# Attention, spectral mixing and feed-forward on one core: one written list from the last attention units to the first up-projection

## The chip, the cores and the metric

The kernel runs on one core of a Trainium2 chip, in one launch. The metric is the device time of that launch in microseconds (us). Five engines work side by side: TensorE (PE: matmuls and transposes; PEld: its weight loads), VectorE (DVE), ScalarE (ACT), GpSimd (POOL) and SyncE (SP, which here issues nearly all DMAs). Each has its own stream of instructions and waits for the others by semaphores.

## The reference, cut to what matters

```python
# attention: B=4, H=8, S=576, D=64
scores = q @ k^T / 8 ;  rel = |i - j|
x = log1p(rel) / log1p(max(i, 1))
bias = relu(x*w1 + b1) @ w2                  # hidden 32, one plane per head
attn = softmax(scores + bias) ; a = attn @ v
# mixing and feed-forward: x = a as (4, 576, 512)
u  = x + real(fft(fft(x, axis=seq), axis=feature))
un = (u - mean(u)) / sqrt(var(u) + 1e-6)
out = u + relu(un @ w_ch1) @ w_ch2           # 512 -> 2048 -> 512
```

## The kernel before, in words

**Bias and attention.** A first phase computes the position bias (up to about 65 us). Then come 16 attention units: a unit is a pair of heads of one batch. A unit has nine blocks of 128 score rows. The work of a unit is cut into lettered tokens: `S` scores on PE; `D` adds the bias and takes the row extreme (a custom DVE instruction, line 290); `X` is the exponential on ACT (298); `T`/`R` are PE transposes of the probabilities, `V` their copies out of PSUM; `A` is the product with v (462), `O` copies its result out; `E` transposes that, `Y` scales it by the inverse sums into `x`; `Q` makes those inverse sums (`Q1`, line 486 and 487, also sends a column to other partitions by a DMA, which in the last two units is issued by ACT); `W`/`U` turn a slice of the feed-forward weights into fp32 and store it in device memory. The lists `ORDER` and `SECOND` fix the order on PE, DVE and ACT; a prime means the unit before.

**The passage.** The last unit, the rests of the units before it, and the mixing of batch 0 follow the list `TAIL`, in which PE, DVE, ACT and POOL all stand in written order. Further tokens there: `p`, `g`, `h` fold the sequence (`pq`, `ge`) and split it into a high and a low part (`gh`, `gl`); `z` is the sequence transform (line 674, `zp`, 8 matmuls), `a`/`b` copy its parts out (`z00h`, `z00l`); `f` is the feature transform (693, `abp`, two times 6 matmuls), `i`, `j`, `k`, `l` join it with `x`; `c` is one column (feature 0) for all batches, made by 18 narrow matmuls (827, `cp`) of which the result `dc` enters `j`; `m`, `n`, `r` are the statistics of the norm and its root; `q` calls the square root once so that ACT's table is loaded there (838). The list ends in `E1' O E1`. After it, code that is not in the list scales batch 0 (`un`, lines 778 on ACT and 781 on DVE), transposes it (`ut`, 795), splits it (`uh` on ACT 797, `ul` on DVE 798), and scales the last attention results.

**The feed-forward.** Then no order is written: a scheduler with its own estimates orders the rest. `dense` runs 16 slices f per batch: split `w1` (high part on ACT 886, low part on POOL 887), load and split `w2`, the up-projection (line 909: 4 blocks of 3 matmuls of 512 columns, for f=0 sorted so that the four with `ul` come last), relu split into `hh`/`hl` (914, 915), and one slice later the down-projection (923: 12 matmuls). The mixing and the norm of the next batch run beside it. Batch b+1's folds (654 to 667) run on DVE. Last comes a half batch of the 64 rest rows of all four batches, whose `w2` low parts are made on DVE. `w2` slices are loaded into three buffers in turn.

Of the kernel before, what the change touches and what calls it, by code (L numbers as in the profile page):

```python
# [20 lines left out]
P = 128  # L21
# [4 lines left out]
ND = 258  # L26
# [9 lines left out]
ON_ACT = set("R0 T00 T01 T03 T04 T10 T11 T12 T13".split())  # L36
# [13 lines left out]
A3'' X8' A4'' S1 X2' X4' E1''' R1' D1 S0 Y1''' R0' Q0' VR1' D0 T10' O'' S2 S4 Q1' D2 VR0' T00' VT10'  # L50
T01' VT00' D4 VT01' S3 T11' S6 T02' D3 D6 VT11' E2'' X3 S7 VT02' Y2'' S8 U0 T13' T12' W0 A0' D7 X6 W1 VT13'
W2 W3 S5 T04' VT12' T03' D8 U1 A1' X7 X0 VT03' VT04' X1 D5 U2 U3 X5 A2'
# [5 lines left out]
S1 D1 S2 T10' D2 S4 T00' VT10' T01' D4 VT00' VT01' S8' S3 T11' VT11' D8' X8' T02' D3 S6 Q0' VT02' D6 S0 R1'  # L58
R0' VR1' X3 VR0' D0 S7 S8 U0 T13' T12' W0 A0' D7 X6 W1 VT13' W2 W3 S5 T04' VT12' T03' D8 U1 Q1' A1' X7 X0
VT03' VT04' X1 D5 U2 U3 X5 A2'  # L60
# [5 lines left out]
E1''' c0 X2' A3'' Y1''' X8' p0 X4' A4'' T11' O'' T10' VT11' S2 p1 VT10' W0 T02' D2 U0 S4 Q0' VT02' R0'  # L66
p2 S7 D4 VR0' p3 T03' D7 S8 VT03' T00' D8 S1 VT00' T12' g0 D1 p5 S5 VT12' E1'' X1 p4 S6 Y1'' X7 T04' Q1'
T01' X8 A0' VT01' X2 h0 A1' VT04' g1 D5 T13' D6 X5 S3 R1' X6 S0 VR1' VT13' A2' X4 D0 D3 X0 T11 h1 z00 X3
q W1 z11 W2 U1 c1 T01 a00 A3' a11 Q0 b11 b00 A4' U2 U3 z10 VT11 Q1 VT01 O' W3 T00 a10 R0 b10 z01 VR0
VT00 R1 a01 c2 b01 VR1 f1 c3 T10 i1 T12 VT10 j1 VT12 E2' f0 k1 l1 Y2' T04 m1 i0 T02 VT04 A0 j0 VT02 n1  # L70
T03 l0 E2'' k0 VT03 A1 T13 Y2'' n0 A2 VT13 m0 A3 r A4 E1' O E1
""".split()
TAIL_ACT = set("""
VR0 VR0' VT00' VT01 VT02 VT03 VT03' VT04 VT04' VT10 VT11 VT11' VT12 VT13 VT13'
""".split())
# [14 lines left out]
def shape_tables():  # L90
# [23 lines left out]
    fd[..., 257:] = 0.0  # L114
    return {
# [17 lines left out]
def body(ctx, tc, a, out):  # L133
# [39 lines left out]
    biasp = pool("biasp", 1, stack=early_)  # L173
    smp = pool("smp", 3, stack=late, side="right")
# [3 lines left out]
    pp = pool("pp", 1, stack=late, side="right")  # L178
# [73 lines left out]
    nms, bank = {}, {}  # L252
# [28 lines left out]
    def largest(n, i):  # L281
        hp, b = units[n]
        blk = (BLK if n else BLK0)[i]
        t = blk % 4 if blk < 8 else 4
        if t not in pt_[n]:
            pt_[n][t] = (pp.tile([P, 2, S], F32, tag="p", name="p", bufs=8) if t < 4
                         else pp.tile([P, S], F32, tag="pr", name="pr", bufs=2))
        bias = bt[hp, t][:, blk // 4] if blk < 8 else bt[hp, 4]
        p, bias = (w.rearrange("p (c s) -> p c s", c=2) for w in (prob(n, blk), bias))
        nc.vector.tensor_tensor_reduce(  # L290
            p, bank.pop((n, i))[:, :, :CH], bias, -0.125, 3.0e38, ALU.add, ALU.min, nms[n][:, blk:blk + 1])
        if b == B - 1 and hp + 1 < HP and blk >= 4:
            load_bias(hp + 1, blk - 4)
# [111 lines left out]
    with ExitStack() as st:  # L405
        ptp = pool("ptp", 1, stack=late, side="right")
        otp = pool("otp", 2, stack=late, side="right")
        rawu = pool("rawu", 1, stack=late, side="right")
# [91 lines left out]
        def scaled(u, w):  # L500
# [14 lines left out]
            "T": turn, "R": turn, "V": lambda u, w: turned(u, w[1:], w[1:] in ON_ACT),  # L515
# [87 lines left out]
        def mix_buffers():  # L603
# [7 lines left out]
            fd = fwp.tile([P, 2, 2, 2, ND], F32R, name="fd")  # L611
# [6 lines left out]
        class Mix:  # L618
# [29 lines left out]
            def fold(self, eng, c, i):  # L648

                if i == 0:  # L650
                    self.buffers(c)
# [17 lines left out]
            def seq(self, c, d):  # L669
                gh, gl = self.g[c]  # L670
                ps = self.ps[c, d] = fps.tile([P, 512], F32, tag="f", name="zp")
# [16 lines left out]
            def feat(self, t):  # L688
                ab = self.ab[t] = [fps.tile([P, 512], F32, tag="f", name="abp") for _ in range(2)]
                for c in range(2):  # L690
                    mm = [(z[c, kb][i][:, 128 * t:128 * t + 128], fd[:, kb, c, j]) for kb in range(2) for i, j in PROD]
# [29 lines left out]
            def pieces(self):  # L721
                eng = nc.vector

                def fold(c):
                    for i in range(3):
                        self.fold(eng, c, i)
                    self.fold_hi(c)
                    self.fold_lo(c)

                def seq(c, d):  # L730
                    self.seq(c, d)
                    self.seq_out(c, d, False)
# [12 lines left out]
                return res + [lambda t=t: feat(t) for t in range(2 + self.b % 2)]

        def norm(tiles, act=False):
# [22 lines left out]
            def scale(i):  # L770
                if not un:
                    un.append(unp.tile([P, n, DM], F32, tag="un", name="un"))
                if act and i < 3:
                    if not i:
# [9 lines left out]
            return un, [lambda i=i: stats(i) for i in range(n)], [root] + [lambda i=i: scale(i) for i in range(n)]  # L784

        def flip(un, n):
            ut = []

            def one_tile(t):
                if not ut:  # L790
                    ut.extend(unp.tile([P, 4, 512], F32R, tag=nm, name=nm) for nm in ("uh", "ul"))
                uh, ul = ut
                ps = (fps if t < 2 else hps).tile([P, 4, P], F32, tag="f" if t < 2 else "h", name="ut")
                for kb in range(4):
                    nc.tensor.transpose(ps[:, kb], un[0][:, t, P * kb:P * kb + P], ident)  # L795
                c = slice(P * t, P * t + P)
                nc.scalar.activation(uh[:, :, c], ps, AF.Copy)
                nc.vector.tensor_tensor(ul[:, :, c], ps, uh[:, :, c].bitcast(F32), ALU.subtract)  # L798

            return ut, [lambda t=t: one_tile(t) for t in range(n)]  # L800

# [5 lines left out]
        un, stats, scales = norm(tl, True)  # L807
        root = scales.pop(0)
        col = {}

        def column(i):
# [6 lines left out]
            elif i == 1:  # L818
                cos = col["cos"] = rawp.tile([P, 3, 384], F32, tag="raw", name="cos")
                hi, lo = (fs[:, :, 0, j].bitcast(F32) for j in range(2))  # L820
                nc.gpsimd.tensor_tensor(cos[:, :, 0:320], hi, lo, ALU.add)
                nc.gpsimd.tensor_tensor(cos[:, :, 320:384], hi[:, :, 256:320], lo[:, :, 256:320], ALU.add)
            elif i == 2:
                ps = col["ps"] = tps.tile([P, 3, B], F32, tag="t", name="cp")
                for t in range(3):
                    for kb, p in enumerate((128, 128, 64)):
                        nc.tensor.matmul(
                            ps[:, t], col["cos"][:p, kb, 128 * t:128 * t + 128], col["x"][:p, kb],
                            start=kb == 0, stop=kb == 2)
            else:  # L830
                ps = col["ps"]
                nc.scalar.activation(dc[:, 0:2], ps[:, 0:2], AF.Copy)
# [199 lines left out]
```

## Time and profile before

| | us |
|---|---|
| median of three runs | 786.39 (784.91 to 787.5) |
| the profiled execution, whole | 785.68 |
| its span (first to last instruction) | 783.8 |
| PE busy in the span | 758.9 (97%) |
| ACT / DVE / POOL busy | 436.6 / 433.3 / 345.8 |

The page's rows give for each line an engine's busy time, the mean of one instruction, and the idle time just before it with what ended that. The rows read from it stand below the change.

### The profile page before, as it was taken

Reading aid. Unit: us, or ns where it says so; the run is one execution under the profiler, and the core shown is the slowest. Engines: PE = TensorE matmul, PEld = TensorE weight load, DVE = VectorE, ACT = ScalarE, POOL = GpSimd, SP = SyncE. Lnnn points to the kernel's source line nnn. Section 1 sums busy time; section 2 is a strip of 40 time slices with the busy share of each in tenths; the row PEclk is TensorE's granted clock in tenths of the full one; section 3 lists DMA queues with packets and bytes.
Section 4 is the critical chain, followed back from the end, with each engine's and each line's share of the span. In section 5 each row is a group of like instructions: output and inputs, shape, how many; then the busy total and the mean of one; then the engine's idle time right before and its main releaser. Section 6 shows DMA issues by size and latency. Waiting matters only on the chain.

```text
span 783.8 us, 13206 instructions
## 1 busy us (share of the span) xinstructions
PE 758.9 (97%) x4786; PEld 618.3 (79%) x4786; DVE 433.3 (55%) x962; ACT 436.6 (56%) x901; POOL 345.8 (44%) x293
## 2 busy tenths in 40 slices
PE   6999899999999999979999999999999999999997
PEld 4567677888778887748888888888888888888896
DVE  7997687887887887579471241712228122111433
ACT  7995888877988888554333333333333333333453
POOL 0003554664465644135554434644345444445342
PEclk9999999999999999989999999999999999999999
DMA  8988989989879842541111131111211113111331
GB/s 217 239 221 231 255 218 275 310 233 281 231 208 295 220 123 82 173 163 41 44 38 54 41 95 45 43 48 45 90 55 30 52 43 105 42 53 55 110 98 62
DMA packets 59488, 103.16 MB, mean 132 GB/s; under 512 B 8768, under 2 KB 28864, under 8 KB 58304
## 3 DMA queue, kind: packets, MB, share of 16 engines
q1 hardware_dynamic: 58672, 98.99, 44.7%
q0 software_dynamic: 288, 3.02, 1.1%
q8 instruction: 37, 0.61, 0.3%
q10 hardware_dynamic: 464, 0.33, 0.1%
q14 instruction: 27, 0.22, 0.1%
HBM read 78.58 MB, written 21.07 MB: 127 GB/s over the span
## 4 chain that ended last, share of the span: by engine, by line
PE 84%; DMA 4%; ACT 3%; DVE 3%; issue 2%; SPq 2%; POOL 1%; ACTq 0%; DVEq 0%
PE hp L909 25%; PE acc L923 25%; PE o L462 9%; PE s L272 9%; PE t L441 6%; PE bps L391 2%; PE abp L693 2%; PE zp L674 2%; DMA bias<-ring 1%; DVE hd L371 1%; SPq L330 1%; ACT p L298 1%; DMA v<-v 1%; PE ut L795 1%; PE t L431 1%
## 5 line engine op out<-in xcount | busy, mean ns | idle before, releaser
L915 DVE SCALAR_TENSOR_TENSOR hl<-hp,hh 128x512 fp32r<-128x512 f32 (+1 forms) x80 | 50.8, 635 | 225.6 <-ACT hh L914 225.6
L887 POOL TENSOR_TENSOR w1l<-w,w1h 128x512 fp32r<-128x512 f32 x80 | 106.2, 1329 | 118.1 <-ACT w1h L886 114.6
L887 POOL TENSOR_TENSOR w2l<-w2f,w2h 128x512 fp32r<-128x512 f32 x64 | 85.0, 1329 | 102.4 <-ACT w2h L886 102.2
L909 PE MATMUL hp<-uh,w1h 128*128 128x512 f32 (+1 forms) x320 | 118.7, 372 | 4.9 <-DVE ul L798 4.9
L909 PE MATMUL hp<-uh,w1l 128*128 128x512 f32 (+1 forms) x320 | 118.6, 371 | 0.0
L290 DVE CUSTOM_DVE_ANT_0 p<-s,bias 128x576 f32<-128x576 f32 x128 | 95.0, 752 | 41.2 <-PE s L272 37.4
L886 ACT ACTIVATE w2h<-w2f 128x512 fp32r<-128x512 f32 x80 | 50.4, 632 | 118.3 <-POOL w1l L887 75.9
L909 PE MATMUL hp<-ul,w1h 128*128 128x512 f32 (+1 forms) x320 | 115.6, 369 | 0.0
L886 ACT ACTIVATE w1h<-w 128x512 fp32r<-128x512 f32 x80 | 50.5, 631 | 114.0 <-PE hp L909 107.8
L923 PE MATMUL acc<-w2l,hh 128*128 128x512 f32 x288 | 112.3, 390 | 0.0
L923 PE MATMUL acc<-w2h,hh 128*128 128x512 f32 x288 | 111.9, 391 | 0.0
L923 PE MATMUL acc<-w2h,hl 128*128 128x512 f32 x288 | 106.9, 391 | 0.0
L272 PE MATMUL s<-kh,qs 128*128 128x288 f32 (+1 forms) x320 | 98.7, 327 | 2.2 <-DVE nm L290 2.0
L298 ACT ACTIVATE p<-p,nm 128x576 f32<-128x576 f32 x128 | 98.1, 772 | 3.0 <-DVE nm L290 1.9
L421 ACT ACTIVATE pt<-t 128x512 f32<-128x512 f32 x141 | 77.7, 594 | 38.4 <-PE t L441 20.0
L272 PE MATMUL s<-kl,qs 128*128 128x288 f32 (+1 forms) x320 | 88.2, 295 | 0.9 <-DVE kl L213 0.9
L462 PE MATMUL o<-pt,v 128*64 128x288 f32 x640 | 86.7, 416 | 0.0
L209 POOL TENSOR_SCALAR kh<-kT 128x576 fp32r<-128x576 f32 (+1 forms) x28 | 22.1, 806 | 146.3 <-PE s L272 124.7
L441 PE MATMUL t<-ident,p 128*128 128x128 f32 x576 | 80.0, 275 | 4.3 <-ACT pt L421 4.1
L272 PEld LDWEIGHTS s<-kh,qs 128*128 128x128 f32 (+1 forms) x320 | 58.4, 183 | 19.3 <-issue 6.6
L909 PEld LDWEIGHTS hp<-uh,w1h 128*128 128x128 f32 x320 | 60.8, 190 | 15.7 <-issue 5.2
L441 PEld LDWEIGHTS t<-ident,p 128*128 128x128 f32 x576 | 66.5, 141 | 8.0 <-ACT pt L421 5.5
(138 smaller groups left out, 1381.3 us busy)
## 6 DMA issues: line engine op xcount, KB each, us to landing
w2f<-w_d SPq DMA_DIRECT2D x80, 256.0 KB, 2.6
raw<-m SPq DMA_DIRECT2D x30, 512.0 KB, 5.1
kT<-kT SPq DMA_DIRECT2D x32, 304.0 KB, 5.4
qT<-qT SPq DMA_DIRECT2D x32, 288.0 KB, 4.6
bias_d<-ring SPq DMA_DIRECT2D x54, 144.0 KB, 2.7
bias<-bias_d SPq DMA_DIRECT2D x24, 288.0 KB, 5.0
v<-v SPq DMA_DIRECT2D x16, 320.0 KB, 6.4
out<-x SPq DMA_DIRECT2D x18, 256.0 KB, 2.7
```

The lines of the kernel that those rows point to most:

```text
L209: nc.gpsimd.tensor_scalar(dst[:, c], src[:, c], 1.0, 0.0, ALU.mult, ALU.add)
L272: nc.tensor.matmul(ps[:m, c, :CH], qs[:, c0:c0 + m], kk[:, k0 + c * CH:k0 + (c + 1) * CH], start=k == 0, stop=k == 1, skip_group_check=True)
L290: nc.vector.tensor_tensor_reduce(p, bank.pop((n, i))[:, :, :CH], bias, -0.125, 3.0e38, ALU.add, ALU.min, nms[n][:, blk:blk + 1])
L298: nc.scalar.activation(p, p, AF.Exp, bias=nms[n][:, blk:blk + 1], scale=-1.0, accum_out=sums[n][:, blk:blk + 1])
L421: nc.scalar.activation(dst, src, AF.Copy)
L441: nc.tensor.transpose(tp[:, 128 * t:128 * t + 128], pb[t].rearrange("p h s -> p (h s)")[:, k0:k0 + 128], ident)
L462: nc.tensor.matmul(os_[u][e, c, :CH], vt[u][:, j, e], pts[u][:, 2 * j + h if j < 4 else 8, c * CH:(c + 1) * CH], start=j == 0, stop=j == 4 ...
L886: nc.scalar.activation(h, src, AF.Copy)
L887: eng.tensor_tensor(l, src, h.bitcast(F32), ALU.subtract)
L909: nc.tensor.matmul(ps[:, :N], (wh, wl)[wi][:, P * kb:P * kb + P], ut[ui][:, kb, :N], start=i == 0, stop=i == len(mm) - 1)
L915: nc.vector.scalar_tensor_tensor(hl[:, :N], ps[:, :N], 0.0, hh[:, :N].bitcast(F32), ALU.max, ALU.subtract)
L923: nc.tensor.matmul(acc[t], h[i][:, P * t:P * t + P], w[j], start=f == 0 and k == 0, stop=f == NF - 1 and k == 2)
```

## The change

1. **The list.** `TAIL` is rewritten and now reaches up to and including the first up-projection of batch 0. New tokens: `u`/`d` scale a tile on ACT or DVE, `t`/`s` transpose it, `G`/`H` take its high and low parts, `B`, `L` and `N` load, split and use the first slice of `w1`. `V` now always means a copy by ACT and `v` one by DVE. One of the folds (`P5`) moves from POOL to DVE.
2. **The column.** It becomes 8 matmuls with `fs` moving (320 wide), a copy of the resulting 16 rows and three small transposes, in place of 18 narrow matmuls and two sums on POOL.
3. **Buffers.** The normalized tokens and their parts live in freed buffers of the probabilities (`pp`); the `w10` slice lives in freed score buffers; `w1` has 16 tiles of its own; `w2` slices have two buffers.
4. **The bias tiles** of the next head pair are asked for at the first `D` of a pair's last batch into two spare tiles, the others in the order in which their buffers come free.
5. **The first batch.** The steps from `w1_parts(1)` to `down(0)` are written out, with the folds of batch 1 between them; VectorE keeps written order through all of the first batch, and the mixing of batch 1 is cut into finer pieces.

```diff
-TAIL = """
-E1''' c0 X2' A3'' Y1''' X8' p0 X4' A4'' T11' O'' T10' VT11' S2 p1 VT10' W0 T02' D2 U0 S4 Q0' VT02' R0'
...
-T03 l0 E2'' k0 VT03 A1 T13 Y2'' n0 A2 VT13 m0 A3 r A4 E1' O E1
+TAIL = """
+X2' A3'' A4'' R1' E1''' O'' S2 c0 X4' vR1' Y1''' E1'' p2 D2 Y1'' S3 T01' D3 S0 X8' T13' VT01' D0 R0' p0 X2 S4 S1
...
+n1 VT02 m1 r A2 A3 u3 d1 A4 E1' t1 O d2 s3 d0 t2 Y1' G1 G3 H1 s0 G2 G0 E2 H3 Y2 E1 Y1 H0 H2 N0
...
-            pt_[n][t] = (pp.tile([P, 2, S], F32, tag="p", name="p", bufs=8) if t < 4
-                         else pp.tile([P, S], F32, tag="pr", name="pr", bufs=2))
+            if t < 4:
+                two = pp.tile([P, 2, 2, S], F32, tag="p", name="p", bufs=4)
+                pt_[n][t - t % 2], pt_[n][t - t % 2 + 1] = two[:, 0], two[:, 1]
+            else:
+                pt_[n][4] = prp.tile([P, S], F32, tag="pr", name="pr")
...
-        if b == B - 1 and hp + 1 < HP and blk >= 4:
-            load_bias(hp + 1, blk - 4)
+        if b == B - 1 and hp + 1 < HP:
+            if not seen:
+                load_bias(hp + 1, 4)
+                load_bias(hp + 1, NEED[0])
+            seen.add(blk)
+            if blk < 8 and (blk + 4) % 8 in seen and len(seen & set(range(8))) < 8:
+                load_bias(hp + 1, NEED[sum(t in seen and t + 4 in seen for t in range(4))])
...
-                cos = col["cos"] = rawp.tile([P, 3, 384], F32, tag="raw", name="cos")
-                hi, lo = (fs[:, :, 0, j].bitcast(F32) for j in range(2))
-                nc.gpsimd.tensor_tensor(cos[:, :, 0:320], hi, lo, ALU.add)
-                nc.gpsimd.tensor_tensor(cos[:, :, 320:384], hi[:, :, 256:320], lo[:, :, 256:320], ALU.add)
+                nc.scalar.activation(h, many, AF.Copy)
+                nc.vector.tensor_tensor(l, many[:, 0:2], h[:, 0:2].bitcast(F32), ALU.subtract)
...
+                ps = col["ps"] = tps.tile([P, 512], F32, tag="t", name="cp")
+                mm = [((col["h"], col["l"])[i], kb, j) for kb in range(2) for i, j in PROD]
+                mm += [(col["h"], 2, 0), (col["h"], 2, 1)]
...
+            elif i == 3:
+                row = col["row"] = rawp.tile([16, 384], F32, tag="raw", name="row")
+                nc.scalar.activation(row[:, 0:320], col["ps"][:16, 0:320], AF.Copy)
+                nc.vector.tensor_copy(row[:, 320:384], col["ps"][:16, 256:320])
+            elif i == 4:
+                ps = col["ps"] = tps.tile([P, 3, 16], F32, tag="t", name="cq")
                 for t in range(3):
...
+                    nc.tensor.transpose(ps[:, t], col["row"][:, P * t:P * t + P], ident[:16, :16])
...
+        def first_up(w):
+
+            if w[0] == "B":
+                k = stp.tile([P, KW], F32R, tag="kh", name="w10")
+                raw, w0["h"] = k[:, 0:512].bitcast(F32), k[:, 512:1024]
+                w0["l"] = stp.tile([P, 2 * S], F32R, tag="qs", name="w10l")[:, 0:512]
+                nc.sync.dma_start(raw, w1_d[0].rearrange("p k c -> p (k c)"))
...
+                mm = [(kb, i, j) for i, j in ((0, 0), (1, 0), (0, 1)) for kb in range(4)]
...
-        w2p = pool("w2p", 3, stack=st)
+        w2p = pool("w2p", 2, stack=st)
...
+            if n_first:
+                for f in range(1, NF):
+                    w1_load(f)
+                    if f < 3:
+                        w2_load(f - 1)
+                w1_load(0)
+                part = lambda i: mix.fold(nc.vector, 0, i)
+                for step, i in (
+                        (w1_parts, 1), (part, 0), (part, 1), (relu_parts, 0), (w2_parts, 0), (part, 2),
+                        (mix.fold_hi, 0), (w1_parts, 2), (up, 1), (mix.fold_lo, 0), (relu_parts, 1), (w2_parts, 1),
+                        (down, 0)):
+                    step(i)
+                fixed.close()
...
+            with ExitStack() as held:
+                if b == 0:
+                    held.enter_context(tc.manual_schedule(engines={DVE_}))
+                run(main, pcs)
```

On VectorE, at the end of the passage before, from the norm's last small step (`nb`) on: `un` is a scaled tile, `ul` the low parts of the transposed tokens, `pq` and `ge` the folds of batch 1, `x<-t` the scaling of the attention's last results.

```order
L776 SCALAR_TENSOR_TENSOR nb<-mv,rs 128x4
L781 TENSOR_SCALAR un<-x,mv,rs 128x512
L507 TENSOR_TENSOR x<-t,rs 128x4x128
L798 TENSOR_TENSOR ul<-ut,uh 128x4x128
L654 TENSOR_TENSOR pq<-x 128x1024
L658 TENSOR_TENSOR ge<-x 128x256
L798 TENSOR_TENSOR ul<-ut,uh 128x4x128
L507 TENSOR_TENSOR x<-t,rs 128x4x128
L798 TENSOR_TENSOR ul<-ut,uh 128x4x128
L656 TENSOR_TENSOR ge<-pq 128x512
L798 TENSOR_TENSOR ul<-ut,uh 128x4x128
L510 TENSOR_TENSOR x<-t,rr 128x128
```

The same place on VectorE now, where `tok` stands for all of the scaled tiles and their parts:

```order
L785 SCALAR_TENSOR_TENSOR nb<-mv,rs 128x4
L790 TENSOR_SCALAR tok<-x,mv,rs 128x512 x3
L517 TENSOR_TENSOR x<-t,rs 128x4x128
L816 TENSOR_TENSOR tok<-ut,tok 128x4x128 x2
L520 TENSOR_TENSOR x<-t,rr 128x128
L517 TENSOR_TENSOR x<-t,rs 128x4x128
L816 TENSOR_TENSOR tok<-ut,tok 128x4x128 x2
L664 TENSOR_TENSOR pq<-x 128x1024
L666 TENSOR_TENSOR ge<-pq 128x512
L973 SCALAR_TENSOR_TENSOR hl<-hp,hh 128x512
L668 TENSOR_TENSOR ge<-x 128x256
```

Three of the four tiles are scaled on VectorE now instead of one, and the folds of batch 1 stand behind all four low parts, `ge<-x` even behind the first relu's low part.

On PE, from the attention's last products (`o`) to the first up-projection (`hp`) before; `t<-ident,ot` are the transposes of the attention's results:

```order
L462 MATMUL o<-pt,v 64x288 x12
L493 MATMUL t<-ident,ot 128x128 x8
L795 MATMUL ut<-ident,un 128x128 x16
L497 MATMUL t<-ident,ot 128x128
L498 MATMUL t<-ident,ot 64x128
L909 MATMUL hp<-uh,w1h 128x512
```

And now, with the first slice's own tiles (`w_4266` its high part, `w10l` its low part):

```order
L451 MATMUL t<-ident,p 128x128 x16
L472 MATMUL o<-pt,v 64x288 x20
L503 MATMUL t<-ident,ot 128x128 x4
L807 MATMUL ut<-ident,tok 128x128 x16
L507 MATMUL t<-ident,ot 128x128
L508 MATMUL t<-ident,ot 64x128
L503 MATMUL t<-ident,ot 128x128 x4
L884 MATMUL hp<-tok,w_4266 128x512 x4
L884 MATMUL hp<-tok,w10l 128x512 x4
L884 MATMUL hp<-tok,w_4266 128x512 x4
```

One group of the transposes of the attention's results moved behind those of the tokens, and the four matmuls with the tokens' low parts end the up-projection as before.

On ACT, in the passage before, around the load of the square root's table:

```order
L838 ACT_TABLE_LOAD
L838 ACTIVATE sq<-ident 128x1
L686 ACTIVATE z00h<-zp 128x320
L686 ACTIVATE z11h<-zp 128x320
L477 ACTIVATE rs<-sm 128x9
L421 ACTIVATE pt<-t 128x512
L487 DMA rr<-rs 64x1 x2
L421 ACTIVATE pt<-t 128x512
L473 ACTIVATE ot<-o 128x576
L686 ACTIVATE z10h<-zp 128x320
```

And now (`row` and `cq` belong to the new column):

```order
L696 ACTIVATE z10h<-zp 128x320
L431 ACTIVATE pt<-t 128x512
L497 DMA rr<-rs 64x1 x2
L852 ACTIVATE row<-cp 16x320
L866 ACT_TABLE_LOAD
L866 ACTIVATE sq<-ident 128x1
L708 ACTIVATE bs<-abp 128x257
L860 ACTIVATE dc<-cq 128x8
L863 ACTIVATE dc<-cq 64x2 x2
L431 ACTIVATE pt<-t 128x512
```

The table load moved from before the first copy of the sequence transform to behind the last one, directly ahead of the feature transform's copy `bs`.

## Rows read from the trace of the kernel before

**Rows 1.** Busy time by stretch: start:end, length, PE, PEld, DVE, ACT, POOL, PEclk, DMA

```profile
284.00:316.00 32.00, 31.43 (x243) 25.27 (x242) 24.58 (x64) 26.45 (x62) 13.59 (x10) 1.00 0.32 92
...
328.67:351.39 22.72, 17.22 (x120) 12.57 (x119) 15.13 (x33) 10.89 (x23) 6.50 (x6) 0.88 0.57 195
```

**Rows 2.** What PE waited for: total us, times, longest

```profile
PE hp L909 <- DVE ul L798: 4.9, 1, 4.9
PE t L441 <- ACT pt L421: 4.1, 4, 2.3
...
PE t L431 <- ACT pt L421: 0.6, 1, 0.6
```

**Rows 3.** Chain of waits, 322 to 362 us: start, us, what

```profile
324.55 1.18 PE zp L674 x8
...
325.98 2.76 PE cp L827 x18
328.74 2.88 PE abp L693 x12
...
333.27 1.44 PE abp L693 x12
334.70 0.87 PE t L441 x8
...
342.88 2.20 ACT un L778 x3
...
345.61 0.49 ACT uh L797
...
346.81 1.23 DVE pq L654
...
351.39 7.64 PE hp L909 x24
```

**Rows 4.** The same chain, 364 to 382 us: one up-projection later on

```profile
369.57 2.72 PE hp L909 x12
```

**Rows 5.** Busy time by single microsecond (columns as in rows 1)

```profile
349.00:350.00 1.00, 0.00 (x0) 0.00 (x0) 1.00 (x3) 0.42 (x1) 0.16 (x1) 0.50 0.06 20
```

**Rows 6.** VectorE in order of time: start, us, what, idle before

```profile
332.07 0.49 DVE L705 SCALAR_TENSOR_TENSOR dm<-abp,dc,bs 128x257 f32<-128x257 f32 x1 [4.99 <-ACT bs L697]
...
337.96 0.28 DVE L510 TENSOR_TENSOR x<-t,rr 128x128 f32<-128x128 f32 x1
...
340.93 0.18 DVE L768 RECIPROCAL rs<-rs 128x4 f32<-128x4 f32 x1
...
353.12 1.22 DVE L654 TENSOR_TENSOR pq<-x 128x1024 f32<-128x1024 f32 x1
354.27 0.69 DVE L666 TENSOR_TENSOR gl<-ge,gh 128x512 fp32r<-128x512 f32 x1
...
355.60 0.42 DVE L658 TENSOR_TENSOR ge<-x 128x256 f32<-128x256 f32 x1
...
360.81 1.51 DVE L658 TENSOR_TENSOR ge<-x 128x256 f32<-128x256 f32 x1
```

**Rows 7.** ScalarE and its queue in order of time

```profile
317.51 1.28 ACT L838 ACT_TABLE_LOAD   x1
318.81 0.20 ACT L838 ACTIVATE sq<-ident 128x1 f32<-128x1 f32 x1
...
322.07 1.12 ACTq L487 DMA_DIRECT2D rr<-rs  x2
...
324.26 0.45 ACT L686 ACTIVATE z10h<-zp 128x320 fp32r<-128x320 f32 x1
...
331.65 0.39 ACT L697 ACTIVATE bs<-abp 128x257 f32<-128x257 f32 x1 [2.47 <-PE abp L693]
```

**Rows 8.** GpSimd in order of time

```profile
358.86 3.18 POOL L887 TENSOR_TENSOR w2l<-w2f,w2h 128x512 fp32r<-128x512 f32 x2
```

**Rows 9.** DMA issues of the page: queue, count, KB each, us to landing

```profile
w2f<-w_d SPq DMA_DIRECT2D x80, 256.0 KB, 2.6
```

More of the change, by code (lines that the diff above doesn't have):

```diff
@@ L35 @@
 FIRST = range(4, 12)
-ON_ACT = set("R0 T00 T01 T03 T04 T10 T11 T12 T13".split())
+NEED = [0, 1, 3, 2]
 N0 = 572
@@ L806, in body @@
         tl = [x[:, 0, t] for t in range(4)]
-        un, stats, scales = norm(tl, True)
-        root = scales.pop(0)
-        col = {}
+        un, stats, root, scale = norm(tl)
+        ut, across, high, low = flip(un)
+        col, w0 = {}, {}
         def column(i):
@@ L844, in body @@
+        small = {
+            "p": lambda i: mix.fold(nc.gpsimd, i // 3, i % 3), "P": lambda i: mix.fold(nc.vector, i // 3, i % 3),
+            "g": mix.fold_hi, "h": mix.fold_lo,
+            "z": lambda c, d: mix.seq(c, d, tps), "Z": mix.seq,
+            "a": lambda c, d: mix.seq_out(c, d, False), "b": lambda c, d: mix.seq_out(c, d, True),
+            "c": column, "f": mix.feat, "F": lambda t: mix.feat(t, hps), "i": mix.feat_b,
             "j": mix.join, "k": lambda t: mix.add(t, True), "l": lambda t: mix.add(t, False),
-            "m": lambda t: stats[t](), "n": lambda t: stats[t + 2](), "q": sqrt_table, "r": root,
+            "m": stats, "n": lambda t: stats(t + 2), "q": sqrt_table, "r": root,
+            "u": lambda t: scale(t, True), "d": scale,
+            "t": lambda t: across(t, fps), "s": lambda t: across(t, hps), "G": high, "H": low,
@@ L917, in up, with layer @@
                 hs[f] = (hh, hl)
+            def layer(f):
+                if f not in w1s:
+                    w1_parts(f)
+                w2_load(f)
+                w2_parts(f)
+                up(f)
+                relu_parts(f)
             def down(f):
@@ L930, in end @@
                     store(t)
+            if n_first:
+                for f in range(1, NF):
[10 more added lines that the diff above has]
+                fixed.close()
             pieces = []
[L933 to L934 removed]
+            for f in range(n_first, NF):
+                pieces.append(lambda f=f: layer(f))
                 if 0 < f < NF - 1:
@@ L945, in run, with prepare, one_tile @@
                 piece()
-        def prepare(b):
-            tl = [x[:, b, t] for t in range(4)]
-            un, stats, scales = norm(tl)
-            return tl, un, Mix(b).pieces() + stats + scales
+        def prepare(tl, mix=None):
+            un, stats, root, scale = norm(tl)
+            n = len(tl)
+            pcs = mix.pieces(mix.b == 1) if mix else []
+            pcs += [lambda i=i: stats(i) for i in range(n)] + [root] + [lambda i=i: scale(i) for i in range(n)]
+            ut, across, high, low = flip(un)
+            def one_tile(t):
+                across(t, fps if t < 2 else hps)
+                high(t)
+                low(t)
+            return tl, ut, pcs, [lambda t=t: one_tile(t) for t in range(n)]
         rest_tiles = [x[:, 0, 4], x[:, 2, 4]]
+        mix = Mix(1)
         for b in range(B):
@@ L955, in store @@
                 nc.sync.dma_start(out[4 * b + t], x[:, b, t])
-            main, last_down, end = dense(ut, tl, store)
+            main, last_down, end = dense(ut, tl, store, 0 if b else 2, mix)
             if b + 1 < B:
-                tl, un, pcs = prepare(b + 1)
-                n = 4
-            else:
-                un, stats, scales = norm(rest_tiles)
-                pcs = stats + scales
-                n = 2
-            run(main, pcs)
-            ut, fl = flip(un, n)
+                tl, ut, pcs, fl = prepare([x[:, b + 1, t] for t in range(4)], mix if b == 0 else Mix(b + 1))
+            else:
+                tl, ut, pcs, fl = prepare(rest_tiles)
+            with ExitStack() as held:
+                if b == 0:
+                    held.enter_context(tc.manual_schedule(engines={DVE_}))
+                run(main, pcs)
             run(fl + last_down)
```

208 lines of the change are left out of this document (112 added, 96 removed).

## The prediction

> **What bounds the kernel now.** I read the stretches first. In all of them but one PE is the limit: in the 32 us before the mixing's last part PE is busy 31.43 of 32.00, ACT 26.45 and DVE 24.58. The exception is the stretch from the feature transform to the first up-projection: 22.72 us with PE busy 17.22, at a mean granted clock of 0.88 [rows 1]. Second, the list of waits shows where PE stood: once for 4.9 us at the first `hp` for a low part `ul`, and otherwise mostly for ACT's copies `pt` at the transposes (4.1 us in four waits, 2.3 the longest; 0.6 at L431) [rows 2]. Third, the chain of waits: the column's product `cp` takes 2.76 us in 18 matmuls; the first feature transform after it takes 2.88, the second, of the same 12 matmuls, 1.44; later scalings on ACT (2.20), a fold of batch 1 (`pq`, 1.23) and the high and low parts stand between the attention's end and the up-projection, and the first two up-projections take 7.64 [rows 3] where one costs 2.72 later on [rows 4]. Fourth, single microseconds give the reason for the doubled prices: after PE had stood idle the granted clock was 0.50 [rows 5], the lower of its two levels (1.2 of 2.4 GHz). So before the first batch some 10 us are lost in which PE idles or runs at half speed, and the change aims at all of them. The sum is made against the profiled execution's 785.68; this lies 0.71 under the median of 786.39, so 0.71 is added at the end.
>
> **The column.** Eight matmuls 320 wide, like the eight of `zp`, which take 1.18, replace 2.76 [rows 3]: gain 1.58. The three small transposes `cq` lie beside ACT's work of that moment. If `cp` came out like the present one, the gain would be 0; better than 1.18 I exclude, as `zp` already runs at full clock.
>
> **From the feature transform to the first up-projection.** Before: from 328.74 to 351.39, 22.65 [rows 3]. Now I follow the written list from the end of the last `zp`. On ACT come `z10h` 0.45, one `pt` copy (taken at 0.5), the two DMA issues 1.12, the row's copy (like `z10h`, 0.45), the table load 1.28 and its first use about 0.1, then `bs` 0.39 [rows 7] and three short copies into `dc`, about 0.5 by the 0.20 of so short an instruction [rows 7]. Allowing for 0.6 in which the issues wait for DVE's inverse sums, that is 5.4 from the end of `zp`. PE starts the feature transform 2.06 after it (1.18 of `cp` and two groups of four transposes at 0.44, half of 0.87 [rows 3]), so the join can begin 3.3 after the transform's start, where it began 3.33 after it before (332.07 [rows 6] less 328.74). DVE's chain from there to the norm's last reciprocal took 332.07 to 341.11, 9.04 [rows 6]; two products like the one at 337.96 (0.28, of which 0.2 counts, as they overlap) now stand elsewhere: 8.6, which ends at 11.9. Then `nb` 0.2; on ACT the scaling `u3` 0.73 (a third of 2.20), the attention's last copy 0.65 and four high parts at about 0.5 [rows 3], 3.5 in all: 15.6. The low parts run beside and the four matmuls that need them come last in the up-projection. So it starts 15.7 after the feature transform's start. PE's own work allows that: 17.22 [rows 1] less 1.44 for the transform at full clock, less 0.88 (eight transposes, 0.87 [rows 3], that now stand ahead of it), is 14.9.
> Gain: 22.65 - 15.7 - 0.88 = 6.1. Its bounds: no better than PE's own work, 22.65 - 14.9 - 0.88 = 6.9; no worse than 3.6, if the join waits 2.5 longer for ACT, whose queue here is all in order, so that `bs`, `dc` and then every `pt` copy (and PE's transposes by them) stand behind the table load and the issues.
> The table load ran 317.51 to 318.79 and its first user began at 318.81 [rows 7], so its price here is 1.28. The Trainium skill, "ScalarE: Activation LUTs", section "What ACT_TABLE_LOAD costs", puts about 2.7 us on a switch of tables, drain included; by that figure, as an estimate, the time would be 1.4 longer than my sum. The row shows no such drain, and I go by it.
>
> **The first up-projection's clock.** The 24 matmuls of the first two took 7.64, at full clock 2 x 2.72 = 5.44 [rows 3, 4]; up to 2.2 is lost. Before, PE had stood 4.9 us [rows 2], which brought the lower clock [rows 5]; with 14.9 of work in 15.7 no gap of more than about 1 us is left. I take 1.9; bounds 0 and 2.2.
>
> **Stalls in the rewritten list.** PE waits for `pt` copies at a few places, 2.3 the longest [rows 2]; the new list interleaves three units on an ACT that is busy 83% (26.45 of 32.00) [rows 1]. Bounds: +0.6, the wait at L431 gone [rows 2], and -2.5, one such wait more. I take -0.8, the price of one ordinary wait (4.1 in four is 1.0 each) in part covered.
>
> **The first batch.** Before, the first low parts of batch 1's folds were made while PE stood. Now `ge<-x` and `gl` follow the first relu on DVE, beside POOL's low parts of `w1` and `w2`. There one fold takes 1.51 instead of 0.42 [rows 6], while POOL's two take 3.18 [rows 8]. PE's `zp` for batch 1 follows the second up-projection, 2.72 after the first [rows 4]; hl 0.7, `ge` 0.4 to 1.5, `gl` 0.7 after relu's 0.6 make 2.4 to 3.5. Bounds 0 and -2.4 (both folds and `pq` held by 1.1 each less the 0.9 of slack); I take -0.4.
> The Trainium skill, "SBUF — State Buffer", section "Who interferes with whom", says that a DVE instruction with two SBUF inputs and a GpSimd instruction that reads SBUF lock one another out. The rows agree (0.42 against 1.51). It speaks against moving the folds behind the relu, and is the base of the third rival's mechanism, which is priced below from rows.
>
> **What costs nothing.** Two `w2` buffers instead of three: a slice lands in 2.6 [rows 9], and its copies take about 1.4 (0.69 for the low part [rows 6], the same for the high one); 4.0 is under two slices of the half batch, 2 x 2.72 [rows 4], the shortest there are; if that cover failed, about 16 slices x 0.5. The earlier bias tiles: PE waited for none, no such wait stands among rows 2, and the program's DMA queue keeps its order. The first slice of `w1` loads and splits while the last unit runs; were it late, its 2.6 and 1.4 would stand at the up-projection. Taking two scalings from ACT to DVE lies in the chain above.
>
> **Sum.** 1.58 + 6.1 + 1.9 - 0.8 - 0.4 = 8.4. 785.68 - 8.4 = 777.3; plus 0.71 gives 778.0. With all good ends 785.68 - 1.58 - 6.9 - 2.2 - 0.6 + 0.71 = 775.1. With two or three bad ends (join late 2.5, clock not returned 1.9, a stall 1.7 more) 778.0 + 2.5 to 6.1 = 780.5 to 784.1.
>
> **Rivals.**
> - *The stall moves (13%).* ACT and DVE set the passage's pace, and what PE no longer waits for at the end it waits for earlier, at `pt` copies and joins: only the column (1.58) and the two clock terms (1.44 and part of 1.9) are gained. For it: ACT's 83% and PE's waits on `pt` [rows 1, 2]. Against: PE was busy 98% in those 32 us, so ACT kept up. 786.39 - 1.58 - 1.44 - 1.0 = 782.4.
> - *The clock stays low (8%).* Were PE to stand again before the up-projection long enough for the lower clock, the 1.9 is not gained: 779.9. For it: ACT's 3.5 behind `nb`, in which PE has few transposes left.
> - *VectorE's written order costs the first batch (9%).* Between two relu parts stand nine folds, gl, gh, ge, ge, pq, gl, gh, ge, ge: with 0.69 for each gl and each long ge, 0.42 for each gh and each short ge, and 1.22 for pq [rows 6], 5.7 us, which is one slice's whole period of 5.44 (2 x 2.72 [rows 4]). Held by POOL each may take 1.1 more [rows 6], together up to 15.5; PE would wait for `hl` in its down-projection for up to 15.5 - 5.44 - 2.7 = 7, and a second, shorter such place costs some 4.7. With 8.4 gained and 11.7 lost: 786.39 - 8.4 + 11.7 = 789.7. It decides when more than 8.4 is lost there. Before, the scheduler placed the relu parts freely. Against: POOL is busy 44% of the span, so about four of nine folds meet it, and then the loss is 1 or nothing.
> - *Nothing of it shows (5%).* If new waits ahead of the transform eat all (`zp` waiting for folds that one more operation on DVE delays), 786.
>
> **How the numbers follow.** My forecast and its own range, 775 to 780.5, has 65%; the low clock lies inside that (8%); the moved stall up to 784 13%; the rest 14%. The range 774.5 to 784 leaves out the third and fourth rivals and little below. What a measurement of this kernel can tell from no change is 0.3%, 2.4 us: faster means under 784.0. Faster: 65 + 8 + 12 = 85%; the same: 6%; slower: 9%.
>
> **What would show it.** Right: PE's wait for `ul` before `hp` gone or under 1.5; `cp` x8 at about 1.2; the first 12 `hp` matmuls at about 2.7 to 3; two feature transforms at 1.44 each; 15 to 17 us from the first of them to `hp`. Wrong: a new PE wait on `bs`, `dc` or `pt` of over 2 us behind the table load; a PE wait on `hl` at `acc` in the first batch; on `gl` at `zp`; or a stretch of 0.50 clock where PE did not stand before. The forecast falls if the stretch up to the transform grows by what the stretch behind it gives.

## The result

The changed kernel takes 776.03 us (median of 4 runs, 773.27 to 776.86) against 786.94 for the kernel before (4 runs): ratio 0.9856, interval 0.9821 to 0.9892, about 11 us faster. Forecast were 778.0, and 774.5 to 784.0 as the range. A later comparison of the same two kernels gives 0.9868 (0.9845 to 0.9892).

Whole runs of one kernel spread by 2 to 10 us, so a place in the kernel is measured within one profile, from a fixed mark: ScalarE's copy `ot` of the thirteenth attention unit, the last that stands in the old lists of both kernels. Its rows, of the kernel before and of the changed one:

```profile
284.83 0.63 ACT L473 ACTIVATE ot<-o 128x576 f32<-128x576 f32 x1
```

```profile
285.51 0.63 ACT L483 ACTIVATE ot<-o 128x576 f32<-128x576 f32 x1
```

From that mark to the first feature transform, the kernel before (one stretch; columns as in rows 1), and then the changed kernel in the same stretch and in the next, up to the first up-projection:

```profile
284.83:328.67 43.84, 42.58 (x321) 34.62 (x319) 31.94 (x81) 32.37 (x74) 15.54 (x12) 1.00 0.34 104
```

```profile
285.51:327.88 42.37, 40.27 (x318) 33.98 (x317) 33.63 (x83) 32.30 (x75) 13.96 (x10) 1.00 0.27 88
...
327.88:343.26 15.38, 14.28 (x116) 10.91 (x114) 14.09 (x35) 9.19 (x21) 3.04 (x4) 1.00 0.45 155
```

So 1.5 us come from the stretch before the transform, although PE idles more there (42.37 - 40.27 = 2.10 against 1.26), and 7.3 from the stretch behind it (15.38 against 22.72 [rows 1]). PE's waits in the changed kernel, over the whole of it as in [rows 2]; the wait for `ul` is gone. Of the 6.5 for `pt` copies 5.9 lie ahead of the mark, as 3.8 of the 4.1 did before; of those for `nm` the longest, 1.4, lies behind it:

```profile
PE t L451 <- ACT pt L431: 6.5, 5, 2.5
...
PE s L271 <- DVE nm L292: 3.9, 6, 1.4
...
PE ut L807 <- DVE tok L790: 0.5, 1, 0.5
...
PE hp L884 <- ACT tok L812: 0.3, 1, 0.3
```

The chain of waits of the changed kernel through the same places, against [rows 3]: start, us, what.

```profile
324.91 1.19 PE zp L684 x8
326.12 0.45 ACT z10h L696
...
327.73 0.62 ACTq L497
328.46 0.43 ACT row L852
328.90 1.28 ACT L866
330.77 0.49 DVE dm L716
...
339.91 0.82 ACT tok L787
340.72 0.54 ACT ot L483
341.26 1.96 ACT tok L812 x4
343.26 3.07 PE hp L884 x12
346.33 2.73 PE hp L964 x12
```

The path has left PE: behind the last `zp` it runs over ScalarE (copy, DMA issue, which waits for VectorE's inverse sums, row, table load `L866`), then VectorE from the join `dm` on, then ScalarE's scaling, copy and high parts. The first up-projection takes 2.91 up to the start of the second where it took 4.75, and the first two now stand at full clock.

Microseconds after the mark, in the profile of every run (its own mark is subtracted; the same program differs by 0.3 from profile to profile):

| run | first `hp` | first store of batch 0 | ratio to the kernel before |
|---|---|---|---|
| before | 66.56 | 166.42 | |
| changed | 57.75 | 155.71 | 0.9856 (0.9821 to 0.9892) |
| after_again | 58.04 | 155.99 | 0.9868 (0.9845 to 0.9892) |
| x_narrow | 59.14 | 157.09 | 0.9890 (0.9866 to 0.9914) |
| x_q_early | 57.83 | 155.77 | 0.9871 (0.9844 to 0.9897) |
| h_q_pool | 57.36 | 155.30 | 0.9888 (0.9865 to 0.9911) |
| x_act3 | 59.02 | 156.96 | 0.9899 (0.9872 to 0.9927) |
| x_dve_free | 57.17 | 158.57 | 0.9921 (0.9896 to 0.9946) |
| x_w2_bias | 57.74 | 155.70 | 0.9869 (0.9842 to 0.9896) |
| x_p5_pool | 55.87 | 153.82 | 0.9833 (0.9809 to 0.9857) |
| h_best | 55.32 | 153.26 | 0.9827 (0.9803 to 0.9850) |
| b_column | 64.25 | 163.76 | 0.9996 (0.9976 to 1.0016) |
| b_fill | 65.05 | 162.96 | 0.9992 (0.9970 to 1.0014) |
| b_bank | 62.98 | 164.92 | 0.9961 (0.9935 to 0.9987) |

By the last column but one the changed kernel gains 10.7 by the first store of batch 0. Of this 10.35 are left where the last stores are issued (495.02 after the mark before, 484.67 now). The whole profiled executions differ by less, 785.68 - 776.84 = 8.84: in this profile the mark itself lies 0.68 later, and the span goes on for 4.92 behind the last issue instead of 3.95; other profiles of the changed list have 3.8 to 5.1 there.

### The profile page after: what moved, and what is told of

It reads as the page before. It is cut to its first block, busy times and chain, and to the rows that moved or that the text cites. A ratio compares the mean times of both kernels' runs of the same rounds, so it can differ in the third digit from the quotient of the medians.

```text
span 775.1 us, 13211 instructions
## 1 busy us (share of the span) xinstructions
PE 750.3 (97%) x4779; PEld 614.0 (79%) x4779; DVE 433.8 (56%) x968; ACT 435.2 (56%) x901; POOL 340.6 (44%) x290
## 3 DMA queue, kind: packets, MB, share of 16 engines
q0 software_dynamic: 288, 3.08, 1.3%
## 4 chain that ended last, share of the span: by engine, by line
PE 85%; DMA 5%; DVE 4%; ACT 4%; issue 1%; ACTq 0%; DVEq 0%; SPq 0%
PE acc L989 25%; PE hp L964 25%; PE s L271 10%; PE o L472 9%; PE t L451 6%; PE bps L400 3%; PE zp L684 2%; DMA raw<-m 2%; DMA bias<-ring 2%; PE abp L704 1%; DVE p L292 1%; ACT p L307 1%; PE ut L807 1%; DMA v<-v 1%; DVE hd L380 1%
## 5 line engine op out<-in xcount | busy, mean ns | idle before, releaser
L964 PE MATMUL hp<-tok,w1h 128*128 128x512 f32 (+1 forms) x632 | 179.6, 368 | 0.0
L933 POOL TENSOR_TENSOR w1l<-w,w1h 128x512 fp32r<-128x512 f32 x79 | 103.1, 1305 | 111.9 <-ACT w1h L932 110.7
L964 PEld LDWEIGHTS hp<-tok,w1h 128*128 128x128 f32 x632 | 115.0, 188 | 20.1
L964 PE MATMUL hp<-tok,w1l 128*128 128x512 f32 (+1 forms) x316 | 116.1, 368 | 0.0
L472 PE MATMUL o<-pt,v 128*64 128x288 f32 x640 | 84.2, 411 | 0.0
L472 PEld LDWEIGHTS o<-pt,v 128*64 128x64 f32 x640 | 43.3, 137 | 30.7 <-issue 4.7
```

Source lines behind the costliest of these rows:

```text
L472: nc.tensor.matmul(os_[u][e, c, :CH], vt[u][:, j, e], pts[u][:, 2 * j + h if j < 4 else 8, c * CH:(c + 1) * CH], start=j == 0, stop=j == 4 ...
L933: eng.tensor_tensor(l, src, h.bitcast(F32), ALU.subtract)
L964: nc.tensor.matmul(ps[:, :N], w[wi][:, P * kb:P * kb + P], ut[ui][:, kb, :N], start=i == 0, stop=i == len(mm) - 1)
```

## The experiments

**after_again: the yardstick.** No edit.

> The changed kernel, unaltered, as the yardstick for the runs beside it: 775 to 777, and from the first feature transform's start to the first up-projection 15.4 us, as in its first profile.

Measured: 774.69, which is 0.3 under what was expected, and 343.05 - 327.67 = 15.4 from the transform to the up-projection, as expected.

**x_narrow: the old column in the new list.**

In short:

```diff
-        mm = [((col["h"], col["l"])[i], kb, j) ...]   # 8 matmuls, 320 wide; row; 3 transposes
+        ps[:, t] += cos[:p, kb, 128 * t:128 * t + 128]^T col["x"][:p, kb]   # 18 matmuls, 4 wide
```

> The changed kernel with the old column: 18 narrow matmuls and two sums on GpSimd, no row copy, no small transposes. Theory (the narrow matmuls cost 2.76 instead of 1.18 and bring the lower clock with them): cp takes 2.7 us or more, the feature transform after it 2.9 instead of 1.45, and the join starts 1 to 2.5 us later (the part that the table load and the DMA issues on ScalarE would have cost anyway is hidden); the whole 1 to 2.5 slower than the changed kernel. Rival A (only the 1.58 counts, the lower clock in the kernel before came from something else): transform at 1.45, 0 to 1 slower. Rival B (the column lies wholly behind ScalarE's queue): join at the same time, no difference.

The chain of this kernel, and one microsecond of its stretches:

```profile
324.05 2.36 PE cp L846 x18
...
326.99 2.50 PE abp L704 x12
```

```profile
328.00:329.00 1.00, 1.00 (x6) 1.00 (x6) 0.96 (x2) 0.00 (x0) 0.00 (x0) 0.50 0.05 14
```

Both parts of the theory are there, if smaller than it had them: the product takes 2.36 instead of 1.25, and about 0.6 behind its end the granted clock falls to 0.50 though PE has no gap, so that the transform takes 2.50 instead of 1.45. The up-projection comes 1.1 to 1.4 later (59.14 against 58.04 and 57.75); the rest was hidden behind ScalarE. Rivals A and B fall.

**b_column: the new column alone in the kernel before.** Edit: `column()` of the changed kernel, and `a01 c2 b01 VR1 c3 f1 c4 c5 T10 i1` in the old list.

> The kernel before with only the new column (8 wide matmuls, row copy, three small transposes). Theory (the narrow matmuls cost 1.58 themselves and 1.44 more by the lower clock that they bring to the feature transform behind them): transform at 1.45 instead of 2.88, the whole 2.5 to 3 faster than the kernel before. Rival A (the lower clock there has another cause): transform still at 2.9, 1.6 faster. Rival B (ScalarE and VectorE set the pace): under 1 faster.

```profile
326.30 1.28 PE cp L830 x8
327.58 1.43 PE abp L693 x12
...
349.36 7.30 PE hp L920 x24
```

The chain shows the column at 1.28 and the transform at full clock, and the up-projection starts 2.3 earlier, a little under the theory. The timed runs don't show it: 0.9996, or 1.9 faster to 1.3 slower; by them alone rival B (under 1) could stand. Part of the reason may stand in the other profiles: with the old column the chain has the transform at 2.88 before, 2.50 in x_narrow, 2.35 in b_bank and 1.64 in b_fill, where the clock did not fall at all, so what the lower clock costs differs from run to run. That doesn't cover the column's own 1.5, and why the timed runs gain so little stays open. In the mean run the column alone is worth at most 1.9.

**b_fill: work for PE in the 4.9 us.**

```diff
+        fill = ops.tile([P, 2, 512], F32, tag="o", name="fill")[:, 0]
+        for i in range(31):
+            nc.tensor.matmul(fill[:, :NK], fs[:, 0, 0, 0, 0:128], fs[:, 0, 0, 0], start=i == 0, stop=i == 30)
```

> The kernel before with 31 matmuls of 320 columns, whose result is not used, on TensorE in the 4.9 us in which it waits for the low part ul. Theory (the first up-projection is at half clock because TensorE stood before it): the granted clock stays at 1.00, the first two up-projections take 5.4 to 5.7 instead of 7.64, the start of the first is not moved, the whole 1.8 to 2.2 faster than the kernel before. Rival (the first up-projection is slow for what it reads, fresh tiles and four matmuls of low parts that come late): 7.6 as before, no gain.

```profile
328.61 2.59 PE cp L827 x18
331.20 1.64 PE abp L693 x12
...
352.56 5.69 PE hp L912 x24
```

The granted clock while that transform ran (columns as in rows 1):

```profile
331.00:332.00 1.00, 1.00 (x9) 0.98 (x10) 0.00 (x0) 0.39 (x3) 0.00 (x0) 1.00 0.98 322
```

The two up-projections take 5.69 instead of 7.64 [rows 3] with nothing else changed for them, and the granted clock is 1.00 throughout: the half clock came from PE's stand. (The 0.9992 is too coarse for the 2 us; its interval reaches from 2.4 faster to 1.1 slower. The 3.5 that this profile gains by the first store hold 1.2 from a transform that happened to keep its clock.)

**b_bank: what the 4.9 us waited for.**

```diff
-                ps = (fps if t < 2 else hps).tile(...)
+                f = (t < 2) != first                    # first batch: exchanged
+                ps = (fps if f else hps).tile(...)
```

> The kernel before, with the PSUM tiles of the transposed tokens exchanged for the first batch only: tokens 0 and 1 go through the pair of tiles that the up-projection uses (hps), 2 and 3 through the other (fps). Theory (the first up-projection, whose first eight matmuls read no low part, waited 4.94 for the low part of token tile 2 only because that still read the PSUM tile in which the up-projection's sum begins): its start follows the last high part, 2.9 to 3.4 earlier; the four matmuls with low parts then wait up to 1 for the last of these; the second up-projection comes 2.0 to 3.0 earlier. Rival (the up-projection waits for the low parts as data, or for the weights' low part on GpSimd): its start is not moved by more than 0.5.

PE in order of time, with the wait before an instruction in brackets:

```profile
348.05 0.50 PE L910 MATMUL hp<-uh,w1h 128*128 128x512 f32 x1 [1.67 <-ACT uh L798]
...
352.44 1.78 PE L910 MATMUL hp<-ul,w1h 128*128 128x512 f32 x5 [1.90 <-DVE ul L799]
```

```profile
354.00:355.00 1.00, 1.00 (x4) 0.78 (x3) 1.00 (x3) 0.95 (x2) 0.00 (x0) 0.50 0.00 0
```

The first up-projection now starts when the last high part is there, 63.0 after the mark instead of 66.6. So most of the wait named `ul` was for a PSUM tile, not for data: the sum began in the tile from which `ul` of token tile 2 was still being taken. The kernel is faster by it (0.9961). But only 1.5 of the 3.6 are left at the first store, and two of the expected sizes were missed. The matmuls with low parts waited 1.90 instead of up to 1, because a fold of batch 1 stands between these parts on VectorE. And the second up-projection, expected 2.0 to 3.0 earlier, ends only 1.5 earlier: after the 1.67 of stand the clock was still full, but 0.9 behind the 1.90 it fell to 0.50, and the matmuls then stood 0.43 apart.

**x_act3: scalings shared as before.** Edit: `u3 d1 ... d2 ... d0` becomes `d3 u1 ... u2 ... u0`.

> The changed kernel with the scalings of the tokens shared as in the kernel before: three on ScalarE, one on VectorE. Theory (ScalarE's queue behind the norm sets the start of the up-projection): the up-projection starts 1.0 to 1.5 later than in the changed kernel (two scalings of 0.73), the whole 1.0 to 1.5 slower, more if the longer stand brings the lower clock. Rival (the transposes or VectorE set it): under 0.5.

```profile
336.28 0.81 ACT tok L787
337.09 0.54 ACT ot L483
337.63 1.41 ACT tok L787 x2
339.04 1.95 ACT tok L812 x4
```

1.0 to 1.3 later (59.02 against 58.04 and 57.75), two scalings of 0.7. ScalarE's queue behind the norm sets the start, as the sum had it.

**x_q_early: the table load moved ahead.** Edit: `q` from behind `F0` to before `a10`.

> The changed kernel with the square root's table loaded before the copy z10h instead of after the row's copy; nothing else moves. Theory (the table load's 1.28 stands in the chain, of which ScalarE's idle 0.58 before z10h can hide that much): the join starts 0.6 to 0.8 earlier, the whole 0.6 to 0.8 faster than the changed kernel. Rival (the chain runs over PE's own work, the feature transform, and the load is hidden): no change, or 0.7 slower because z10h comes later.

No change (57.83). VectorE in order of time ahead of the join, in the changed kernel:

```profile
329.53 0.68 DVE L165 SCALAR_TENSOR_TENSOR uf<-uf,raw 128x512 int32<-128x512 int32 x1
330.77 0.49 DVE L716 SCALAR_TENSOR_TENSOR dm<-abp,dc,bs 128x257 f32<-128x257 f32 x1 [0.56 <-ACT dc L860]
```

And in this run, ScalarE's copy and then VectorE:

```profile
326.60 0.42 ACT L696 ACTIVATE z10h<-zp 128x320 fp32r<-128x320 f32 x1
```

```profile
328.04 0.69 DVE L165 SCALAR_TENSOR_TENSOR wf<-wf,raw 128x512 int32<-128x512 int32 x1
...
329.98 0.67 DVE L165 SCALAR_TENSOR_TENSOR uf<-uf,raw 128x512 int32<-128x512 int32 x1
330.59 0.49 DVE L716 SCALAR_TENSOR_TENSOR dm<-abp,dc,bs 128x257 f32<-128x257 f32 x1
```

In the changed kernel the join `dm` waited 0.56 for ScalarE when VectorE was free. The load ahead of `z10h` makes that copy 0.7 later (41.35 after the mark instead of 40.61), and with it VectorE's `z10l` and all that stands behind it in written order: three weight conversions, a `pt` copy and the row's rest. That uses up the 0.56, and the join now starts with no gap behind them. The rival's later `z10h` is there; that it reaches the join by VectorE's queue neither theory nor rival had.

**h_q_pool: also the small DMAs off ScalarE.** Edit: for the last two units `nc.gpsimd` issues them instead of `nc.scalar`.

> The early table load as in the run beside it, and the two last units' small column DMAs issued by GpSimd's queue instead of ScalarE's, which takes 1.12 of issue off ScalarE between z10h and the row's copy. Theory: the join is then bound by the row's copy, the three small transposes and the feature transform itself; it starts 1.0 to 1.8 earlier than in the changed kernel, the whole 1.0 to 1.8 faster. Rival: the copies pt and the PE work bound it, then no more than the run with the early load alone.

0.4 earlier at the up-projection (57.36), which is hardly more than the 0.3 between equal programs, and not the 1.0 to 1.8 of the theory; VectorE's queue binds in the same way.

**x_p5_pool: the moved fold back on GpSimd.** Edit: `P5` becomes `p5`. It follows from these rows of the changed kernel, VectorE, GpSimd and PE:

```profile
307.03 2.31 DVE L668 TENSOR_TENSOR ge<-x 128x256 f32<-128x256 f32 x1
```

```profile
306.69 2.38 POOL L664 TENSOR_TENSOR pq<-x 128x1024 f32<-128x1024 f32 x1
```

```profile
310.08 0.40 PE L271 MATMUL s<-kh,qs 128*128 128x288 f32 x1 [1.41 <-DVE nm L292]
```

> The changed kernel with the one fold that the change moved from GpSimd to VectorE put back on GpSimd, at the same place of the list. Theory (beside GpSimd's own folds the 0.42 of this fold took 2.31 on VectorE, the score blocks behind it came late and TensorE stood 1.41): the wait of 1.41 is gone, and the feature transform and the first up-projection come 1.0 to 1.4 earlier against the steady units before. Rival (the wait only moves: the later chain over ScalarE and VectorE sets the end of the passage): under 0.3.

The wait is gone, PE's idle time from the mark to the transform falls from 2.10 to 0.52, and the up-projection comes 1.9 earlier (55.87), 0.5 more than the wait itself and more than the theory had (equal programs differ by 0.3). The kernel takes 772.53, ratio 0.9833. GpSimd does the fold in 0.74 between two of its own, without a gap:

```profile
308.35 0.74 POOL L668 TENSOR_TENSOR ge<-x 128x256 f32<-128x256 f32 x1
```

**h_best: the three together, and VectorE's conversions moved.** Edit: `p5`; `W3` behind `b00`; `q a10 VT00 U2 b10`; the small DMAs by GpSimd.

> The changed kernel with that fold on GpSimd, the square root's table loaded before z10h, the two small column DMAs on GpSimd's queue, and two of VectorE's three weight conversions that stood between z10l and the join moved ahead of z10l into its idle 1.0. Theory (the join waits for VectorE's conversions once ScalarE is free): the join starts 0.6 to 0.9 earlier beside the 1.0 to 1.4 of the fold, 1.6 to 2.3 in all against the changed kernel. Rival (the join is bound by the feature transform and the small transposes behind it): only the fold's gain.

```profile
324.25 1.47 PE abp L704 x12
...
326.24 0.49 DVE dm L716
...
338.73 3.06 PE hp L884 x12
```

The join starts 2.2 behind the transform's first matmul (326.24 - 324.01), 2.9 in the changed kernel (330.77 - 327.88), and the up-projection 55.32 after the mark: 2.4 to 2.7 better than the changed kernel, 0.55 of it beyond the fold. 771.95, ratio 0.9827, is the lowest median here; the timed runs can't tell it from x_p5_pool.

**x_dve_free: VectorE's order in the first batch back to the scheduler.** Edit: the `manual_schedule(engines={DVE_})` around `run(main, pcs)` left out.

> The changed kernel with VectorE's written order in the rest of the first batch given back to the scheduler; the written steps up to the first down-projection stay. Theory (the order is hidden behind TensorE): the batch takes the same 95 us, the whole the same within 0.5. Rival (the prediction's third: the written order costs the first batch): 1 or more faster. Other side: the scheduler's order makes TensorE wait for hl or a fold, 1 or more slower.

```profile
PE acc L989 <- DVE hl L973: 2.1, 1, 2.1
```

The other side came: from the up-projection to the first store 101.4 instead of 98.0, and the kernel loses more than a third of the gain (0.9921 against 0.9868). VectorE in order of time, of the same kernel:

```profile
350.40 1.40 DVE L677 TENSOR_TENSOR gh<-ge,gh 64x256 fp32r<-64x256 f32 x1
351.84 1.66 DVE L666 TENSOR_TENSOR ge<-pq 128x512 f32<-128x512 f32 x1
353.42 0.41 DVE L668 TENSOR_TENSOR ge<-x 128x256 f32<-128x256 f32 x1
353.76 1.21 DVE L664 TENSOR_TENSOR pq<-x 128x1024 f32<-128x1024 f32 x1
354.89 0.68 DVE L973 SCALAR_TENSOR_TENSOR hl<-hp,hh 128x512 fp32r<-128x512 f32 x1
```

The scheduler put a run of folds of batch 1, three of them held beside GpSimd to 1.4 to 1.8 each, ahead of the low part `hl` for which the down-projection waits: the mechanism of the prediction's third rival, but in the order that was not written. PE stands for 2.6 of the 3.4.

**x_w2_bias: two hidden parts undone.** Edit: `bufs=3` for `w2p`, and the old rule for the bias tiles.

> The changed kernel with three buffers for the w2 slices again and the bias tiles asked for by the old rule. Theory (both were hidden): from the first batch on the same to 0.3 and no new wait of VectorE for a bias tile; the whole the same within 1. Rival (the early bias tiles, or the two buffers, carry part of the gain or a loss): 1 or more slower, or faster, with a wait that shows it.

Same to 0.01 at both places; VectorE waits for bias tiles only ahead of 66 us, in both. Together the two parts are worth nothing here; neither was undone alone.

## Why the prediction was right

It named the right places and nearly the right sizes; 10.7 were gained up to the first store where 8.4 were summed. The first up-projection comes 8.8 earlier; the runs that undo or add one part put 3.6 (b_bank), 2.3 (b_column; 1.1 to 1.4 by x_narrow) and 1.0 to 1.3 (x_act3) to single parts, and the rest is not separated.

- *The column* (1.58): `cp` went from 2.76 to 1.25. Right, and x_narrow shows that only part of it lies in the path, while the clock that it keeps up adds the rest.
- *From the transform to the up-projection* (15.7): 15.38, and it took 22.72 before. The chain ran as written: the join 2.9 behind the transform's start (3.3 forecast), VectorE's part from the join to the norm's last reciprocal 330.77 to 339.62, 8.85 (8.6 forecast), ScalarE's part 339.91 to 343.26, 3.4 (3.5 forecast). What the prediction left open is what PE's 4.9 had waited for; b_bank shows a PSUM tile.
- *The clock* (1.9): 4.75 to 2.91, so 1.84; b_fill shows the cause. For the transform's 2.88 the prediction had the wrong reason: it put both doubled prices down to PE's standing, and ahead of the transform PE stood once, for 0.63, 4.8 us earlier; in b_column it stood there for 0.75, and the clock stayed full. That the transform would come down to 1.44 came true because the new column took away the narrow matmuls: the transform ran at full clock in all ten profiles with the new column, and in part at half clock in three of the four without it.
- *Stalls in the rewritten list* (0.8): PE's idle time ahead of the transform rose by 0.84. The size was right by luck, for the cause was not: it was no `pt` copy but one fold on VectorE beside GpSimd, and of the 4.1 of waits from which the term was read [rows 2] only 0.3 lie behind the mark. The prediction weighed that contention for the folds behind the first relu and not for `P5`, for which the same rows spoke [rows 6].
- *The mis-sized term* is PE's own work ahead of the transform. The sum had 1.58 - 0.88 = 0.70 less; it fell by 42.58 - 40.27 = 2.31. Counted in the timelines from the start of each matmul to the next, without waits, the column gave 1.44 of that, the products `o` 0.46 (10.61 to 10.15), the scores 0.33 (11.64 to 11.31) and the transposes 0.31 (12.57 to 12.26), though eight more stand there, for which the sum had 0.88 to pay; the sequence transform took 0.23 more. What these have in common is that the new list keeps kinds of matmul together: `o` stands in three groups (8, 32, 40) where it stood in six, the scores in 13 where they stood in 15. The chain of the kernel before has a price for a change of kind: eight `o` in a group took 1.12, 0.140 each, twenty-four 3.08, 0.128 each; four transposes behind such a group took 0.59, amid others 0.44. That the grouping is the cause is argued from these rows; no run changes the groups alone.
- *The first batch* (0.4 lost): 95.11 before, 95.05 now from the second up-projection to the store. Nothing is lost, and x_dve_free shows that the written order prevents a loss of 3.4 here: the third rival had the sign wrong.
- *Nothing for `w2`, bias tiles*: as forecast.

Of the rivals, "the stall moves" was true at one place and for 1.4, which one letter undoes.

The Trainium skill, "ScalarE: Activation LUTs", section "What ACT_TABLE_LOAD costs", puts a switch of tables at about 2.7 us with its drain. In the changed kernel the load stands in the chain at 328.90 with 1.28, directly behind the row's copy, and its first user starts at 330.19, so no drain shows and the row decides again. The Trainium skill, "SBUF — State Buffer", section "Who interferes with whom", has the contention of a two-input VectorE instruction with a GpSimd instruction that reads SBUF. It cost 1.41 of PE's time here, in a place where I had not looked for it, and the trace agrees: the fold took 0.42 alone [rows 6] and 2.31 beside GpSimd's 2.38.

## What to carry to other kernels

A wait is named after the last instruction that releases it, not after the thing needed: if the first matmul behind a wait doesn't read the named result, look for a PSUM tile or buffer that is still being read. Where several engines' queues end close to each other, undoing one is worth at most what the next leaves, and less if the change also moves what the next one starts from, so look at what stands directly ahead of the join on each of them: 0.56 lay between VectorE and ScalarE at `dm`, and x_q_early used it up itself. Before a small elementwise operation goes from GpSimd to VectorE, check what GpSimd runs beside it: 0.42 became 2.31, and PE paid.

## What had not been expected

- Narrow matmuls can bring the lower clock without any gap on PE: 18 with 4 columns each (2.4 to 2.8 us) went with a clock of 0.50 in three of four profiles that have them. It fell 2.3 us behind their start before, 2.9 in x_narrow and 3.2 in b_bank; in the fourth (b_fill) it stayed at 1.00. In x_narrow PE has no gap for the 6 us ahead of them; in the other three it waited 0.6 ahead of the last `zp`.
- The length of PE's stand alone doesn't say whether the clock falls: 4.9 brought 0.50 [rows 2, 5], 1.67 (b_bank) and 2.12 (x_dve_free) left 1.00, but 1.90 in b_bank, 2.5 us behind the 1.67, was followed by 0.50. In x_dve_free, behind its 2.12:

```profile
356.00:357.00 1.00, 1.00 (x6) 0.83 (x5) 0.63 (x2) 0.00 (x0) 1.00 (x2) 1.00 0.00 0
```

- Several us of the spread between runs lie ahead of the passage: with the changed list the mark falls between 281.9 and 285.7, with the old one between 284.8 and 287.5, though what stands ahead of it is nearly the same. ScalarE waits in its written order for the raw weights' DMA, and PE for ScalarE's `pt` copies; in the changed kernel's profile, waits of ScalarE up to the mark:

```profile
ACT uf L162 <- DMA raw<-m: 9.4, 3, 3.9
```

In the profile with the earliest mark (x_dve_free, 281.9) this sum is 5.5, in that with the latest (b_fill, 287.5) 9.3; but x_w2_bias has 5.3 with a mark at 285.6, so this wait is not the whole of it, and its part in the spread is not shown. It is a lead for a further change, which was not tried.
